# An mLSTM cell with a mixture-of-depths layer on one core: a scatter moved ahead of a weighing, a mask in halves, a shorter ranking chain, a last layer in two column halves

## The chip, the cores and the metric

The kernel runs on one core of a Trainium2 chip. The metric is the time of one execution in microseconds (us) of the device; several executions are taken and their median counts. The profile is that of one further execution.

## What is computed

The reference, cut to what matters (B = 4 batches, H = 8 heads, S = 768 positions, D = 40, F = 1024, capacity 128, all float32):

```python
for t in range(S):                       # mLSTM cell, per batch and head
    m_new = np.maximum(f_gate[:, :, t] + m, i_gate[:, :, t])
    f_stab = np.exp(f_gate[:, :, t] + m - m_new); i_stab = np.exp(i_gate[:, :, t] - m_new)
    C = f_stab * C + i_stab * outer(vt, kt);  n = f_stab * n + i_stab * kt
    y[:, :, t] = sigmoid(o_gate[:, :, t]) * (C @ qt) / np.maximum(np.abs(n @ qt), 1.0)
x = y.transpose(0, 2, 1, 3).reshape(B, S, H * D)
scores = x @ w_gate                      # mixture of depths, per batch
top_idx = np.argpartition(-scores[b], 128)[:128]
ye = np.maximum(x[b, top_idx] @ w1, 0.0) @ w2
out[b] = x[b];  out[b, top_idx] += sigmoid(scores[b, top_idx])[:, None] * ye
```

## The kernel before

**Steps.** The sequence is cut into 12 steps of 256 positions, three for a batch, numbered 0 to 11 (`N = 12`). A step holds four blocks of 64 positions: `c` is the half of 128 positions on the partitions, `r` the half of 64 within it. For each step the main loop transposes k and q on PE (`turn`, L244, copied out of PSUM by ACT), multiplies v by gate factors on POOL (`weigh`, L260: two instructions, one for `r = 0`, one for `r = 1`), forms the new states on PE (`update`, L282; added up on DVE in `states`), the scores (`scores`, L309), the masked scores on DVE (`masked`, L323), the part of the output that comes from the states (`read`, L332) and the part within a block (`attend`, L362), both into one PSUM tile `pH`. `divide` (L370) makes y on DVE, `output` (L390) multiplies it by the sigmoid of the output gate on POOL, `store` (L397) writes rows of `out`, `router` (L404) takes their score on DVE.

**The second part**, once per batch `b` when its three steps have scores: `spread` (L433) copies all 768 scores to every partition (PE, then ACT into `sb`); `compare` (L486) counts for each position how many scores are greater. Three of the six counts are made by DVE with a comparison, three by ACT with the sum of signs; `halved` (L483) turns a sum of signs s into the count (767 - s)/2. A row is chosen where its count is below 128, and its count is its place. For batches 0 to 2 `fetch` (L546) gathers the chosen rows from `out` in memory by an indirect DMA of POOL (into `xe`), `fetched` (L553) transposes them, `layer1` (with `last_rows`) and `layer2` (L600) are the two matrix products, `weighed` (L608) multiplies by the sigmoid of the score that `valued` (L565) computes, and `add` (L618) adds the result to the rows in `out` by an indirect DMA that accumulates: **the scatter**. For the last batch `picked` (L512) builds 0/1 matrices `sel_f` on DVE (count equal to place) and picks the rows by matmuls, already transposed; `fetch(3)` still gathers the plain rows, which are added on DVE, and its scatter writes without accumulating.

**Order.** It is written out by hand (`manual_schedule`): an engine executes its instructions in the order of the code. The main loop runs steps 0 to 11; at step 9 `layers` (L652) interleaves the second part of batches 0 and 1 with the step and with what step 10 needs (`weigh(10)`, `weigh(11)`, `add(0)`, `turn(10, ..)`, `update(10)`, and the ranking of batch 2). In step 10 come `numbers(2)`, `output(9, (0,))`, `fetch(2)`, `masked(10)`, `output(9, (1,))`, `update(11)`, `states(11)`, `router(9)`, `read(10)`, the transposition of q of step 11, eight sigmoids of the output gates on ACT, `attend(10)`; in step 11 `scores`, `masked`, `router(10)`, `read`, `fetched(2)`, `attend`. Behind the loop (L827 on) stand the second part of batch 2 and that of batch 3, the last scatter, and a test of flags whose register value is read on every engine. POOL's queue carries `weigh`, `output`, most stores, the gathers and the scatters; SP's carries the loads, the last of which (the output gates) are issued until 108.35 us.

A DMA on POOL's queue that touches `out` waits for earlier ones that touch the same rows: the wait of `fetch(2)` names `add(0)`, that of `add(2)` names `add(1)`, that of `fetch(3)` names `add(2)`.

Of the kernel before, what the change touches and what calls it, by code (L numbers as in the profile page):

```python
# [26 lines left out]
def _fast(ctx, tc, q, k, v, i_gate, f_gate, o_gate, w_gate, w1_in, w2_in, out):  # L27
# [105 lines left out]
    iota = const.tile([128, 128], FP, name="iota")  # L133
    id_i = const.tile([128, 2 * NS], I32, name="id_i")
# [15 lines left out]
    def tables():  # L150

        POOL.iota(iota_i, pattern=[[1, 128]], channel_multiplier=0)
        POOL.tensor_copy(out=iota, in_=iota_i)
        for c in range(2):
            POOL.iota(id_i[64 * c:64 * c + 64], pattern=[[256, NS], [64, 2]], base=128 * c, channel_multiplier=1)
        POOL.memset(ones, 1.0)
        POOL.memset(place, 1.0)
        for s in range(NS):
            POOL.memset(place[:, 2 * s:2 * s + 2, 0:1], 256.0 * s)
            POOL.tensor_copy(out=place[:, 2 * s:2 * s + 2, 1], in_=id_i[:, 0:2])  # L160
# [162 lines left out]
    def masked(n):  # L323
        P = work.tile([128, 2, 2, NP, 64], FP, name="P")
        flat = "s j c p t -> s (j c p) t"
        DVE.tensor_tensor(out=P.rearrange(flat), in0=pending[n].pop("pS").rearrange(flat), op=OP.mult,  # L326
                          in1=mask.unsqueeze(1).to_broadcast([128, 4 * NP, 64]))
        pending[n]["P"] = P

    def head(n, p, j):  # L330
        return 2 * p + j if n in APART else NP * j + p
# [30 lines left out]
    def attend(n):  # L362
        g = pending[n]
        for p in range(NP):
            for j in range(2):
                for c in range(2):
                    h = head(n, p, j)
                    g["add"](c, h, g["pH"][64 * c:64 * c + 64, h], g["P"][:, j, c, p, :], wv_t[n % 3][:, c, 2 * p + j], True)
# [62 lines left out]
    def half(b):  # L431
        return slice(128 * (b % 2), 128 * (b % 2) + 128)
# [50 lines left out]
    def halved(d):  # L483
        DVE.tensor_scalar(out=d["cnt"][:, NS:], in0=d["cnt"][:, NS:], scalar1=-0.5, scalar2=0.5 * (S - 1),
                          op0=OP.mult, op1=OP.add)
# [25 lines left out]
    def picked(b):  # L511
# [3 lines left out]
        for r in (slice(0, 3), slice(3, 6)):  # L515
            DVE.tensor_tensor(out=sel[:, r], in0=iota.unsqueeze(1).to_broadcast([128, 3, 128]),
                              in1=d["cnt"][:, r].unsqueeze(2).to_broadcast([128, 3, 128]), op=OP.is_equal)
# [47 lines left out]
    def valued(b):  # L565
        d, xe = dep[b], xe_t[b % 2]
        scr = work.tile([128, DM], FP, name="scr", bufs=1)
        sg = mod.tile([128, 1], FP, name="sg")
        DVE.tensor_tensor_reduce(out=scr, in0=xe[:, 0:DM], in1=wg, scale=1.0, scalar=0.0, op0=OP.mult, op1=OP.add,  # L569
                                 accum_out=sg)  # L570
        d["g"] = mod.tile([128, 1], FP, name="g")
        ACT.activation(out=d["g"], in_=sg, func=AF.Sigmoid)
# [34 lines left out]

    def weighed(b):  # L608

        d = dep[b]  # L610
        d["yg"] = mod.tile([128, DM], FP, name="yg")
        if b == B - 1:
            DVE.scalar_tensor_tensor(out=d["yg"], in0=d["py"], scalar=d["g"], in1=xe_t[b % 2][:, 0:DM], op0=OP.mult, op1=OP.add)
            return
        ACT.activation(out=d["yg"], in_=d["py"], func=AF.Copy, scale=d["g"])
# [48 lines left out]
    def layers(n):  # L664
# [36 lines left out]
        weigh(n + 1)  # L701
        weigh(n + 2)
        add(0)
# [135 lines left out]
    layer1(b - 1, 0)  # L839
    dep[b] = {"sb": spread(b, 0, 2 * NS, ps_u)}  # L840
# [4 lines left out]
    halved(dep[b])  # L845
    valued(b - 1)
# [17 lines left out]
    layer2(b)  # L864
    value = nc.values_load(good[0:1, 0:1], min_val=0, max_val=1)
    weighed(b)
# [353 lines left out]
```

## Time and profile before

| | |
|---|---|
| times of 3 executions | 152.1, 152.0, 151.44 us; median 152.0 us |
| the profiled execution: its own time | 150.96 us |
| its span, first to last instruction | 149.1 us |
| granted clock of TensorE, mean | 0.997 |
| busy: PE, PEld, DVE, ACT, POOL | 138.1, 121.2, 96.0, 99.5, 97.4 us |
| DMA queues' packets, share of 16 engines | SP's and ACT's 65.0%, POOL's 18.8% |

Of the span 149.1 us, 1.9 us of the execution's own time lie outside it. The times below are those of the profiled execution, counted from the start of its span. PE is the matmul side of TensorE and PEld its weight load, which overlaps it. An engine's row in the timeline merges neighbours of one kind; "[1.10 <-DVE P L326]" behind a row says how long the engine stood idle before it and whose end released it. A wait for several semaphores is named after the one that came last by the profile, which is not always the real one.

### The profile page before, as it was taken

How to read it: one execution, taken by the hardware profiler on the slowest of the kernel's cores; microseconds unless marked ns; L12 is line 12 of the kernel's file. 1: busy time of each engine (PE TensorE's matmuls, PEld its weight loads, DVE VectorE, ACT ScalarE, POOL GpSimd, SP SyncE). 2: the span in 40 equal slices, each digit the busy share in tenths (PEclk: the TensorE clock that was granted, in tenths of full speed). 3: DMA queues.
4: the chain of work that ended last, by engine and by line, in shares of the span. 5: the costliest groups of instructions: out<-in, count | busy, mean ns of one | idle time of the engine just before them, and what ended most of it. 6: DMA issues, size and time to landing. Idle time of an engine off the chain costs nothing.

```text
span 149.1 us, 6088 instructions
## 1 busy us (share of the span) xinstructions
PE 138.1 (93%) x2560; PEld 121.2 (81%) x2560; DVE 96.0 (64%) x249; ACT 99.5 (67%) x191; POOL 97.4 (65%) x128
## 2 busy tenths in 40 slices
PE   6999899999999999999999999999999799999930
PEld 7888789989879989988897986997789698799710
DVE  6469496379998597986999924562884976611010
ACT  0656864889797989997978653996977909422100
POOL 7519199969993699399986029499955669431220
PEclk9999999999999999999999999999999999999998
DMA  3999999998999899999989999999991004903101
GB/s 71 206 169 185 133 176 175 172 178 159 190 186 162 159 228 265 181 171 179 314 278 315 317 163 206 225 180 283 188 172 41 7 4 88 211 13 44 53 13 48
DMA packets 80294, 24.27 MB, mean 163 GB/s; under 512 B 75937, under 2 KB 78498, under 8 KB 80258
## 3 DMA queue, kind: packets, MB, share of 16 engines
q1 hardware_dynamic: 77568, 16.78, 65.0%
q0 software_dynamic: 2496, 6.88, 18.8%
q8 instruction: 22, 0.36, 1.1%
q10 hardware_dynamic: 194, 0.13, 0.3%
q14 instruction: 14, 0.11, 0.3%
HBM read 19.20 MB, written 4.59 MB: 160 GB/s over the span
## 4 chain that ended last, share of the span: by engine, by line
PE 39%; DMA 16%; ACT 13%; issue 10%; POOL 9%; DVE 6%; POOLq 2%; ACTq 1%; SPq 1%; DVEq 0%
PE pH L344 8%; PE pt L253 8%; PE pU L288 5%; PE py L606 4%; DMA k<-in_k_dram 4%; PE pS L320 4%; DMA xe<-out_dram,idx 4%; ACT qT L257 3%; DMA v<-in_v_dram 3%; POOL x L394 3%; DMA out_dram<-yg,idx 3%; PE pU L594 3%; DMA i_sb<-in_i_gate_dram 2%; PE ph L594 2%; ACT sgn L474 2%
## 5 line engine op out<-in xcount | busy, mean ns | idle before, releaser
L265 POOL TENSOR_TENSOR wv<-v,cols 64x656 f32<-64x656 f32 x23 | 30.9, 1345 | 15.8 <-DMA v<-in_v_dram 6.7
L394 POOL TENSOR_TENSOR x<-y,so 128x320 f32<-128x320 f32 x24 | 22.2, 934 | 5.8 <-ACT so L271 1.9
L409 DVE CUSTOM_DVE_ANT_0 scr<-x,wg 128x320 f32<-128x320 f32 x22 | 17.8, 808 | 9.0 <-POOL x L394 7.7
L271 ACT ACTIVATE so<-o 64x320 f32<-64x320 f32 x48 | 22.5, 468 | 1.0
L257 ACT COPY qT<-pt 128x512 f32<-128x512 f32 x24 | 13.8, 638 | 9.1 <-PE pt L253 9.1
L606 PE MATMUL py<-w,hT 128*128 128x320 f32 x64 | 18.2, 434 | 0.0
L288 PE MATMUL pU<-wv,k 128*64 128x82 f32 x384 | 16.5, 237 | 0.3 <-POOL wv L265 0.2
L300 DVE TENSOR_TENSOR C<-pU,C 128x164 f32<-128x164 f32 x40 | 13.1, 328 | 5.1 <-PE pU L288 3.8
L255 ACT COPY kT<-pt 128x512 f32<-128x512 f32 x24 | 13.0, 589 | 5.0 <-PE pt L253 4.7
L288 PEld LDWEIGHTS pU<-wv,k 128*64 128x64 f32 x384 | 14.5, 137 | 2.2 <-issue 1.1
L320 PE MATMUL pS<-qT,kT 40*64 40x64 f32 x768 | 14.8, 222 | 1.1 <-issue 0.6
L469 DVE TENSOR_SCALAR_CACHE_REDUCE cmp<-sb,x 128x768 f32<-128x768 f32 x12 | 12.1, 1009 | 5.4 <-ACT sb L463 5.1
L606 PEld LDWEIGHTS py<-w,hT 128*128 128x128 f32 x64 | 11.8, 190 | 4.3
L320 PEld LDWEIGHTS pS<-qT,kT 40*64 40x64 f32 x768 | 12.8, 134 | 2.7 <-issue 1.0
L344 PE MATMUL pH<-wv,P 128*64 128x82 f32 x352 | 15.0, 237 | 0.0
L326 DVE TENSOR_TENSOR P<-pS,mask 128x1024 f32<-128x1024 f32 x12 | 14.6, 1217 | 0.4 <-PE pS L320 0.4
L344 PEld LDWEIGHTS pH<-wv,P 128*64 128x64 f32 x352 | 13.2, 136 | 1.8 <-issue 1.2
L253 PE MATMUL pt<-ident,k 128*128 128x128 f32 x96 | 13.6, 280 | 0.4 <-DMA k<-in_k_dram 0.3
L401 POOL DMA_DIRECT2D out_dram<-x x22 | 13.6, 624 | 0.3 <-POOL x L394 0.3
L549 POOL DMA_INDIRECT xe<-out_dram,idx x4 | 4.4, 1095 | 14.5 <-DVE sg L569 7.8
L253 PE MATMUL pt<-ident,qw 128*128 128x128 f32 x96 | 13.0, 279 | 0.3 <-ACT qw L237 0.2
L232 ACT COPY Z<-C 64x656 f32<-64x656 f32 (+1 forms) x18 | 12.6, 698 | 0.2
(149 smaller groups left out, 244.3 us busy)
## 6 DMA issues: line engine op xcount, KB each, us to landing
k<-in_k_dram SPq DMA_DIRECT2D x24, 160.0 KB, 5.6
q<-in_q_dram SPq DMA_DIRECT2D x12, 320.0 KB, 5.5
v<-in_v_dram SPq DMA_DIRECT2D x24, 160.0 KB, 5.2
out_dram<-x POOLq DMA_DIRECT2D x22, 160.0 KB, 4.9
o<-in_o_gate_dram POOLq DMA_DIRECT2D x12, 160.0 KB, 5.6
o<-in_o_gate_dram SPq DMA_DIRECT2D x12, 160.0 KB, 4.2
w<-in_moe_w_dram SPq DMA_DIRECT2D x8, 160.0 KB, 5.8
w<-in_moe_w_dram SPq DMA_DIRECT2D x4, 256.0 KB, 5.4
```

Of the source, the lines that this page charges most:

```text
L253: PE.transpose(pt[:, p, :], src[:, c, 2 * p:2 * p + 2, :].rearrange("s j d -> s (j d)"), ident)
L257: ACT.copy(out=T.rearrange("e p (u t) -> e t p u", t=2)[:, c], in_=pt)
L265: (DVE if n == 0 and r else POOL).tensor_tensor(out=wv_t[n % 3][o, :, :, r], in0=v_t[n % NB][o], op=OP.mult, in1=cols[s][o, 0:2, b * H:b * ...
L271: ACT.activation(out=so_t[n % 3][64 * c:64 * c + 64, r], in_=o_t[n % NO][64 * r:64 * r + 64, c], func=AF.Sigmoid)
L288: PE.matmul(pU[64 * j:64 * j + 64, c, p], k_t[n % NB][:, c, 2 * p + j, :], wv_t[n % 3][:, c, 2 * p + j], start=True, stop=True)
L320: PE.matmul(pS[o, j, c, p, :], kT[e, p, t], qT[e, p, t], start=True, stop=True)
L326: DVE.tensor_tensor(out=P.rearrange(flat), in0=pending[n].pop("pS").rearrange(flat), op=OP.mult, in1=mask.unsqueeze(1).to_broadcast([128, ...
L344: PE.matmul(o, lhs, rhs, start=(c, h // 4) not in begun, stop=last, skip_group_check=True)
L394: POOL.tensor_tensor(out=x_t[b % 2][:, 2 * s + r, 0:DM], in0=pending[n]["y"][:, r].rearrange("s h d -> s (h d)"), in1=so_t[n % 3][:, r].re ...
L401: (POOL if n < N - 1 else SP).dma_start(out=out[b, a:a + 128, :].rearrange("(r t) d -> t r d", t=64), in_=x_t[b % 2][64 * c:64 * c + 64, 2 ...
L409: DVE.tensor_tensor_reduce(out=scr, in0=x[:, r, 0:DM], in1=wg, scale=1.0, scalar=0.0, op0=OP.mult, op1=OP.add, accum_out=x[:, r, DM:DM + 1])
L606: PE.matmul(d["py"], hT_t[:, f, half(b)], w2[:, f, :], start=(f == 0), stop=(f == NF - 1))
```

## The change

1. In `layers`, `add(0)` stands between `weigh(10)` and `weigh(11)` instead of behind both.
2. At step 11 the mask is multiplied in two instructions, one for the heads with `j = 0` and one for `j = 1`, and `attend` takes all heads of `j = 0` first.
3. In the last ranking `halved` is dropped: the three sums of signs are compared with a second table `margin` = 767 - 2 * place, made by one more POOL instruction at step 0, in place of `iota`. The product of `valued(2)` on DVE (gathered rows times `w_gate`) stands ahead of the comparisons instead of behind them; its sigmoid stays on ACT behind the last sum of signs.
4. `layer2` of batch 3 is computed as two halves of 160 columns in two PSUM tiles, and each half has its own multiply-and-add on DVE, which now stands ahead of the register read.

```diff
@@ tables()
         POOL.tensor_copy(out=iota, in_=iota_i)
+        POOL.tensor_scalar(out=margin, in0=iota, scalar1=-2.0, scalar2=float(S - 1), op0=OP.mult, op1=OP.add)
@@ masked(n)
-        flat = "s j c p t -> s (j c p) t"
-        DVE.tensor_tensor(out=P.rearrange(flat), in0=pending[n].pop("pS").rearrange(flat), op=OP.mult,
-                          in1=mask.unsqueeze(1).to_broadcast([128, 4 * NP, 64]))
+        flat, pS = "s j c p t -> s (j c p) t", pending[n].pop("pS")
+        for j in (slice(0, 1), slice(1, 2)) if n == N - 1 else (slice(0, 2),):
+            w = 2 * NP * (j.stop - j.start)
+            DVE.tensor_tensor(out=P[:, j].rearrange(flat), in0=pS[:, j].rearrange(flat), op=OP.mult,
+                              in1=mask.unsqueeze(1).to_broadcast([128, w, 64]))
@@ attend(n)
-        for p in range(NP):
-            for j in range(2):
-                for c in range(2):
...
+        order = [(p, j) for p in range(NP) for j in range(2)]
+        for p, j in sorted(order, key=lambda x: x[1]) if n == N - 1 else order:
+            for c in range(2):
...
@@ picked(b)
-        for r in (slice(0, 3), slice(3, 6)):
-            DVE.tensor_tensor(out=sel[:, r], in0=iota.unsqueeze(1).to_broadcast([128, 3, 128]),
+        for r, of in ((slice(0, 3), iota), (slice(3, 6), margin)):
+            DVE.tensor_tensor(out=sel[:, r], in0=of.unsqueeze(1).to_broadcast([128, 3, 128]),
                               in1=d["cnt"][:, r].unsqueeze(2).to_broadcast([128, 3, 128]), op=OP.is_equal)
@@ new function
+    def layer2_last(b):
+
+        d, w = dep[b], DM // 2
+        d["yg"] = mod.tile([128, DM], FP, name="yg")
+        for i in range(2):
+            if i == 0:
+                py = ps_t.tile([128, 512], FP, name="py", tag="t")[:, 0:w]
+            else:
+                py = ps_h.tile([128, 2, 512], FP, name="py", tag="h")[:, 0, 0:w]
+            for f in range(NF):
+                PE.matmul(py, hT_t[:, f, half(b)], w2[:, f, w * i:w * i + w], start=(f == 0), stop=(f == NF - 1))
+            DVE.scalar_tensor_tensor(out=d["yg"][:, w * i:w * i + w], in0=py, scalar=d["g"],
+                                     in1=xe_t[b % 2][:, w * i:w * i + w], op0=OP.mult, op1=OP.add)
@@ layers(n)
         weigh(n + 1)
+        add(0)
         weigh(n + 2)
-        add(0)
@@ behind the loop
     layer1(b - 1, 0)
+    total = valued(b - 1, False)
     dep[b] = {"sb": spread(b, 0, 2 * NS, ps_u)}
...
     compare(b, 5, 6)
-    halved(dep[b])
-    valued(b - 1)
+    valued_gate(b - 1, total)
...
-    layer2(b)
+    layer2_last(b)
     value = nc.values_load(good[0:1, 0:1], min_val=0, max_val=1)
-    weighed(b)
     add(b)
```

On POOL, from `weigh(10)` (wv_92) to `fetch(2)`, with the semaphores that each instruction waits for. DMASW0 to DMASW7 count the landings of POOL's own DMAs; `fetch(1)` and `fetch(2)` are on DMASW1, `add(0)` is on DMASW0. Before:

```order
L265 TENSOR_TENSOR wv_92<-v_96,cols 64x16x41 [waits DMAHW7_49,DMAHW0_49,PE_49]
L265 TENSOR_TENSOR wv_92<-v_96,cols 64x16x41 [waits DMASW1_49]
L265 TENSOR_TENSOR wv_93<-v_97,cols 64x16x41 [waits DMAHW5_49,DMAHW4_49,PE_49]
L265 TENSOR_TENSOR wv_93<-v_97,cols 64x16x41
L619 DMA out_dram<-yg,idx_1490 768x320 [waits Pool_49]
L394 TENSOR_TENSOR x_181<-y,so_102 128x320 [waits DVE_49,Activation_49]
L549 DMA xe_178<-out_dram,idx_2053 128x320 [waits DMASW4_49,DMASW3_49,DMASW5_49,DMASW2_49,DMASW6_49,DMASW0_49,DMASW7_49,DVE_49,PE_49]
```

The same place in the changed kernel:

```order
L267 TENSOR_TENSOR wv_92<-v_96,cols 64x16x41 [waits DMAHW7_49,DMAHW0_49,PE_49]
L267 TENSOR_TENSOR wv_92<-v_96,cols 64x16x41 [waits DMASW1_49]
L640 DMA out_dram<-yg,idx_1492 768x320 [waits Pool_49]
L267 TENSOR_TENSOR wv_93<-v_97,cols 64x16x41 [waits DMAHW5_49,DMAHW4_49,PE_49]
L267 TENSOR_TENSOR wv_93<-v_97,cols 64x16x41 [waits DMASW0_49]
L398 TENSOR_TENSOR x_182<-y,so_102 128x320 [waits DVE_49,Activation_49,Pool_49]
L553 DMA xe_179<-out_dram,idx_2055 128x320 [waits DMASW4_49,DMASW5_49,DMASW3_49,DMASW6_49,DMASW2_49,DMASW7_49,DVE_49,PE_49]
```

The scatter (L619, now L640) stands two weighings earlier. The wait for its landing, DMASW0, stood at `fetch(2)` and now stands at the second instruction of `weigh(11)` (wv_93).

On DVE, from the scores of step 11 (`router_last`, the ISA row on x_181) to the 0/1 matrices of the last batch. Before:

```order
L424 ISA x_181<-y,ow 128x320 [waits DVE_49,Pool_49]
L469 TENSOR_SCALAR cmp,cnt<-sb_2309,x_181 128x768 [waits Activation_49]
L469 TENSOR_SCALAR cmp,cnt<-sb_2309,x_181 128x768 [waits DVE_49] x2
L484 TENSOR_SCALAR cnt<-cnt 128x3 [waits Activation_49]
L569 ISA scr,sg<-xe_178,wg 128x320 [waits DMASW1_49]
L516 TENSOR_TENSOR sel_f<-iota,cnt 128x384 [waits DVE_49] x2
```

The same place in the changed kernel:

```order
L428 ISA x_182<-y,ow 128x320 [waits DVE_49,Pool_49]
L573 ISA scr,sg<-xe_179,wg 128x320 [waits DMASW1_49]
L473 TENSOR_SCALAR cmp,cnt<-sb_2315,x_182 128x768 [waits Activation_49]
L473 TENSOR_SCALAR cmp,cnt<-sb_2315,x_182 128x768 [waits DVE_49] x2
L520 TENSOR_TENSOR sel_f<-iota,cnt 128x384 [waits DVE_49]
L520 TENSOR_TENSOR sel_f<-margin,cnt 128x384 [waits Activation_49]
```

The halving (L484) is gone, the product for `valued(2)` (L569, now L573) stands ahead of the comparisons, and only the second of the two 0/1 matrices waits for ACT.

## Rows read from the trace of the kernel before

**Rows 1.** Timeline of PE, steps 10 and 11 and the tail: start us, us, instruction
```profile
110.05 1.35 PE L288 MATMUL pU<-wv,k 128*64 128x82 f32 x32
...
113.43 1.36 PE L344 MATMUL pH<-wv,P 128*64 128x82 f32 x32
...
118.34 1.36 PE L344 MATMUL pU<-wv,P 128*64 128x82 f32 x32 [1.10 <-DVE P L326]
119.63 1.16 PE L583 MATMUL ph<-xeT,w1c 64*128 64x128 f32 x16
...
125.05 4.47 PE L606 MATMUL py<-w,hT 128*128 128x320 f32 x16
129.36 4.15 PE L524 MATMUL pX<-sel_f,x 128*67 128x128 f32 x36
...
134.68 2.05 PE L594 MATMUL pU<-xeT,w 128*128 128x128 f32 x16
136.57 1.95 PE L594 MATMUL ph<-xeT,w 128*128 128x128 f32 x16
...
138.58 4.57 PE L606 MATMUL py<-w,hT 128*128 128x320 f32 x16
```
**Rows 2.** Timeline of DVE, the same stretch
```profile
115.14 0.49 DVE L409 CUSTOM_DVE_ANT_0 scr<-x,wg 128x320 f32<-128x320 f32 x1 [1.88 <-POOL x L394]
...
117.07 1.22 DVE L326 TENSOR_TENSOR P<-pS,mask 128x1024 f32<-128x1024 f32 x1
...
128.35 1.02 DVE L516 TENSOR_TENSOR sel_f<-iota,cnt 128x384 f32<-128x384 f32 x2
...
143.19 0.55 DVE L613 SCALAR_TENSOR_TENSOR yg<-py,g,xe 128x320 f32<-128x320 f32 x1 [4.18 <-PE py L606]
```
**Rows 3.** Timeline of POOL, steps 9 and 10 and the last gather
```profile
101.50 5.37 POOL L265 TENSOR_TENSOR wv<-v,cols 64x656 f32<-64x656 f32 x4
107.15 1.71 POOL L619 DMA_INDIRECT out_dram<-yg,idx  x1 [0.28 <-DVE C L300]
...
113.11 1.11 POOL L549 DMA_INDIRECT xe<-out_dram,idx  x1 [2.81 <-PE pt L253]
114.23 0.88 POOL L394 TENSOR_TENSOR x<-y,so 128x320 f32<-128x320 f32 x1
...
138.14 1.09 POOL L549 DMA_INDIRECT xe<-out_dram,idx  x1 [3.56 <-issue]
```
**Rows 4.** Line L549 from 104 to 116 us: waits of POOL's sequencer, ns min/median/max
```profile
L549 POOLq EVENT_SEMAPHORE  x4: 43/43/3414, 108.7 to 112.3; - x4
```
**Rows 5.** DMA issues around 107, 133 and 138 us: last number, us to landing
```profile
out_dram<-yg,idx POOLq DMA_INDIRECT x1, 5.1
...
out_dram<-yg,idx POOLq DMA_INDIRECT x1, 4.1
...
xe<-out_dram,idx POOLq DMA_INDIRECT x1, 3.1
```
**Rows 6.** Timeline of ACT between the steps' last sigmoids and the gathered rows
```profile
114.28 3.89 ACT L271 ACTIVATE so<-o 64x320 f32<-64x320 f32 x8
118.20 0.54 ACT L562 COPY xeT<-pX 64x128 f32<-64x128 f32 x2
```
**Rows 7.** Queues 106.1:107.1, 108.9:110 (SP's), 90:91.3 (POOL's): packets, MB, share of 16 engines
```profile
q1 hardware_dynamic: 441, 0.07, 42.2%
...
q1 hardware_dynamic: 1386, 0.22, 114.8%
...
q0 software_dynamic: 44, 0.16, 57.8%
```
**Rows 8.** Groups by line and shape, whole span: busy us, mean ns | idle before
```profile
L265 POOL TENSOR_TENSOR wv<-v,cols 64x656 f32<-64x656 f32 x23 | 30.9, 1345 | 15.8 <-DMA v<-in_v_dram 6.7 <-DVE cols L204 4.7 <-PE pH L344 3.6
L153 POOL CAST iota<-iota_i 128x128 f32<-128x128 int32 x1 | 0.3, 289 | 0.1
...
L300 DVE TENSOR_TENSOR C<-pU,C 128x164 f32<-128x164 f32 x40 | 13.1, 328 | 5.1 <-PE pU L288 3.8
```

More of the change, by code (lines that the diff above doesn't have):

```diff
@@ L133, in _fast @@
     iota = const.tile([128, 128], FP, name="iota")
+    margin = const.tile([128, 128], FP, name="margin")
     id_i = const.tile([128, 2 * NS], I32, name="id_i")
@@ L363, in attend @@
         g = pending[n]
-        for p in range(NP):
-            for j in range(2):
-                for c in range(2):
-                    h = head(n, p, j)
-                    g["add"](c, h, g["pH"][64 * c:64 * c + 64, h], g["P"][:, j, c, p, :], wv_t[n % 3][:, c, 2 * p + j], True)
+        order = [(p, j) for p in range(NP) for j in range(2)]
+        for p, j in sorted(order, key=lambda x: x[1]) if n == N - 1 else order:
+            for c in range(2):
+                h = head(n, p, j)
+                g["add"](c, h, g["pH"][64 * c:64 * c + 64, h], g["P"][:, j, c, p, :], wv_t[n % 3][:, c, 2 * p + j], True)
     def divide(n):
@@ L563, in fetched, with valued @@
         ACT.copy(out=d["xeT"][:, 0:2], in_=pX[:, 0:2])
-    def valued(b):
+    def valued(b, gate=True):
         d, xe = dep[b], xe_t[b % 2]
@@ L570, in valued, with valued_gate @@
                                  accum_out=sg)
+        if gate:
+            valued_gate(b, sg)
+        return sg
+    def valued_gate(b, sg):
+        d = dep[b]
         d["g"] = mod.tile([128, 1], FP, name="g")
@@ L611, in weighed @@
         d["yg"] = mod.tile([128, DM], FP, name="yg")
-        if b == B - 1:
-            DVE.scalar_tensor_tensor(out=d["yg"], in0=d["py"], scalar=d["g"], in1=xe_t[b % 2][:, 0:DM], op0=OP.mult, op1=OP.add)
-            return
         ACT.activation(out=d["yg"], in_=d["py"], func=AF.Copy, scale=d["g"])
```

## The prediction

> **What bounds the kernel now.** All four edits lie behind 101 us, so I read only that stretch, engine by engine, PE first. The timeline of PE [rows 1] shows one gap worth naming in steps 10 and 11: 1.10 us before the attention matmuls of step 11, which wait for the mask on DVE. From 118.34 us on every PE row begins where the one before ends, down to the last layer two at 138.58: the reader is to see that PE alone sets the end there. The timeline of DVE [rows 2] leads further back: the mask begins at 117.07 behind step 10's division, and that chain begins with a score product at 115.14 that waited 1.88 us for POOL. POOL's timeline [rows 3] shows why: its product at 114.23 stands behind the gather of batch 2, which began at 113.11 after 2.81 us of idleness. The row blames a PE transposition, but the sequencer's own wait, 3.41 us from 108.7 [rows 4], ends where the first scatter lands: 107.15 + 5.1 = 112.25 [rows 3, 5]. So the chain is scatter, gather, product, score, division, mask, PE. ACT runs beside it: eight sigmoids, then the copies of the gathered rows, done at 118.74 [rows 6], 0.89 us before PE first reads them at 119.63 [rows 1].
>
> **Edit 1, the scatter.** Removed: the first scatter behind four weighings. Moved: it is issued after two. The four take 5.37 us [rows 3], so two end at 101.50 + 2.69 = 104.19; with the gap of 0.28 that it has now it starts at 104.47 and its issue, 1.71 us, ends at 106.18. But the order of the changed kernel puts the wait for its landing at the second half of step 11's weighing, which had no such wait. That half takes 1.345 us [rows 8], and PE's update of step 11, at 110.05 now [rows 1], needs it; in that update's shadow stand, on PE, everything to the end. With a landing after L us the half ends at 104.47 + L + 0.05 + 1.345 and PE starts 0.05 us later (hand-overs of about 0.05 us are my choice from the gaps between neighbouring rows): PE stalls L - 4.14 us before the update.
>
> L is the unknown. The nearest rows are the same kind of scatter: 5.1 us where it is now, 4.1 us for the third one, with no other traffic [rows 5]. Below 4.1 nothing in the trace reaches for an accumulating scatter; above 5.1 the traffic of SP's loads could drive it. Now its data must go between 108.86 and 112.25, beside loads that ask for 114.8% of the engines [rows 7]; moved, its data comes due about 106.6, in a lull in which the loads take 42.2% [rows 7], before they fill up again. The gather of batch 1 also shows that POOL's packets are not starved beside loads: they took 57.8% of the engines [rows 7]. I take 4.6, the middle of the two rows: landing 109.07, second half done 110.47, PE stalled 0.46 us.
>
> What the stall meets: PE has 1.10 us of idleness ahead of step 11's attention. Moved by 0.46, the work before it ends at 118.34 - 1.10 + 0.46 = 117.70. The chain on DVE is no longer late: POOL's product ends about 110.47 + 1.0 + 1.4 + 0.9 = 113.8 (product, gather with its hand-over, product) instead of 115.11, and then PE's attention of step 10, 0.46 later than its 113.43 + 1.36 = 114.79 [rows 1], releases the division at about 115.3. Now the division begins behind the score product, about 115.55 (115.14 + 0.49 less the overlap of neighbours); so the mask starts some 0.2 earlier, at 116.85. **Edit 2** splits it: one instruction of 1.22 us becomes two; with the fixed part that a short DVE instruction shows, some 0.17 us, each is 0.17 + 1.05/2 = 0.70. The first half ends at 117.55, before PE needs it at 117.70; the second at 118.2, before PE has done the first half's heads. Bounds of edit 2: without it the mask would end at 118.05 and PE would wait 0.35 us, so it is worth 0 to 0.55, the latter if PE came early enough; it costs DVE 0.1 us, hidden behind attention.
>
> Next late is ACT: its sigmoids follow a PE transposition that is also 0.46 later, so the gathered rows are ready at 118.74 + 0.46 = 119.20, and PE goes on at about 119.25, not at 119.63. **Gain of edits 1 and 2: 0.4 us**; in general 0.85 less the stall, that is 4.99 - L: 0.85 at best, 0 at L = 5.0, a loss of 0.85 at 5.85.
>
> **Edit 3, the ranking.** Dropped on DVE: a halving (under 0.2 us) and, from this place, a product of 0.5 us. But the two 0/1 matrices are made from 128.35 to 129.37 and PE's picking begins at 129.36, directly behind a layer two that began at 125.05 and runs at its usual pace [rows 1, 2]; the first matrix is ready half a microsecond before. PE covers this: 0 taken, up to 0.3 if PE comes early by more than that half. The product now runs beside POOL's last outputs and may hold one up for its own length, 0.5 us; that ends in the last gather, which lands at 138.14 + 3.1 = 141.24 [rows 3, 5] and is needed at 143.19 [rows 2], by the first half of edit 4 at 141.0. A late gather by 0.5 still lets the second half go on time: 0. The new table is one POOL instruction, 0.29 us by the cast of the same size [rows 8], at step 0; POOL idles for loads of v after it (6.7 us in all [rows 8]): 0.
>
> **Edit 4, the last layer two.** Now 16 passes in 125.05 to 129.36, 0.269 us each at 320 columns [rows 1]; passes of 128 columns with a weight load each come every (136.57 - 134.68)/16 = 0.118 us [rows 1]. Between them, 160 columns: 0.118 + 0.151 x 32/192 = 0.143; 32 of them take 4.58 instead of 4.30: +0.28, or +0.20 with the pace of the picking, 4.15/36 = 0.115 [rows 1]. I take +0.25. The multiply-and-add behind it shrinks from 0.55 [rows 2] to about 0.35, near the 0.328 of a 164-column addition out of PSUM [rows 8]: -0.20. **Net +0.05**, between -0.05 and +0.1. The Trainium skill, "TensorE: Matmul & The Clock Gate", section "The mechanism", says that a weight load overlaps matmuls in flight only where the row groups differ; these all use all rows, and by its section "LDWEIGHTS" 128 columns cost about 107 ns, so 16 more loads would be 1.7 us, an estimate. The row at 0.118 us a pass, load included, disagrees.
>
> **Sum.** -0.40 + 0 + 0.05 = -0.35 us on the profiled execution: 150.96 becomes 150.6. The median of the runs stands 1.04 higher, at 152.0, so **151.65 us**. A measurement tells changes over 0.5%, 0.76 us, from none.
>
> **Rivals.** *The wait is free.* If the scatter lands within 4.2 us, the second half of the weighing hardly waits, the stall is nil and ACT's 0.85 us is the gain: 151.2. For it: the lull. Against: 4.1 is the row with all engines idle. The Trainium skill, "DMA: Bandwidth & Descriptors", section "Anatomy of one DMA", gives a fixed 2.0 us and bytes at 436 GB/s: 2.4 us for these 164 KB, an estimate, and the wait would be free; the scatters' rows, 4.1 and 5.1, say otherwise. Chance 0.15, and 0.07 for gains that I do not see, as a DVE chain at the tail that counted after all.
> *The wait replaces the gain.* One mechanism, on POOL between the two halves of step 11's weighing: the scatter comes into the loads' second burst (114.8% [rows 7]) and lands after 5.8 us or more, so PE stalls 1.7 us before the update, over all its cover. It decides from L = 5.0, and is measurable from 5.8: 152.9. For it: at 107.15 the scatter took 1.0 more than the idle one, though its last third ran when the loads were done. Chance 0.13.
> *Weight loads uncovered in edit 4* at one pass pitch each, 16 x 0.118 = 1.9 us: 153.5, chance 0.03.
> *The scatter isn't where the chain hung*, and edits 1 and 2 do nothing but cost a stall inside 1.10: 152.0 to 152.1, part of the 0.62 that I give to the forecast with L between 4.2 and 5.7.
>
> **How the numbers follow.** Faster 0.22, same 0.62, slower 0.16. The cases reach from 151.1 (free wait, 152.0 - 0.85 - 0.05) to 152.9 (the late scatter); the three runs of before lie 0.66 apart, and nearly all of that below their median, so I add 0.3 below: range 150.8 to 152.9.
>
> **What would show it.** The scatter starts near 104.5 and lands near 109; the second half of the weighing starts there, not at 107.5; PE shows an idle of about half a microsecond before the update of step 11, blamed on POOL, and none of 1.10 before step 11's attention; the picking still begins where layer two ends; 32 passes of 160 columns last about 4.6 us, and the last DVE instruction about 0.35. A PE gap over 1.3 us before the update would prove the forecast wrong on the slow side, none at all on the fast side.

## The result and the profile after

The changed kernel takes **153.4 us** (median of 22 executions, 151.62 to 158.6) against 151.79 for the kernel before beside it (22 executions): ratio 1.0117, 95% interval 1.0091 to 1.0144. It is 1.2% slower; 151.65 was forecast, and 153.4 lies above the range. The ratios here and below leave out executions over 1.5% above the fastest of their kernel (nine of these 22, 154.43 to 158.6 us at a mean granted clock of 0.955 to 0.979), so beside a kernel whose times fall in two groups I give the median as well. The profiled execution takes 152.92 us, its span is 151.2 us at a clock of 0.992 (before: 150.96, 149.1, 0.997).

PE's timeline, the rows that answer to [rows 1]: start us, us, instruction, and in brackets the idleness before it with what ended it.

```profile
106.58 1.35 PE L290 MATMUL pU<-wv,k 128*64 128x82 f32 x32
...
110.89 0.31 PE L547 MATMUL pi<-place,sel 128*128 128x3 bf16 x6 [0.62 <-DVE sel L501]
112.04 1.35 PE L290 MATMUL pU<-wv,k 128*64 128x82 f32 x32 [0.84 <-POOL wv L267]
...
115.42 1.36 PE L348 MATMUL pH<-wv,P 128*64 128x82 f32 x32
...
118.71 0.52 PE L563 MATMUL pX<-ident,xe 128*64 128x128 f32 x3
119.16 1.61 PE L348 MATMUL pU<-wv,P 128*64 128x82 f32 x32
120.70 1.24 PE L593 MATMUL ph<-xeT,w1c 64*128 64x128 f32 x16
...
126.20 4.47 PE L616 MATMUL py<-w,hT 128*128 128x320 f32 x16
130.51 4.15 PE L528 MATMUL pX<-sel_f,x 128*67 128x128 f32 x36
...
139.72 4.61 PE L628 MATMUL py<-w,hT 128*128 128x160 f32 x32
```

The first row is step 10's update. It began at 105.33 before, so 1.25 us were gone ahead of every edit but the new table; over the profiles of all kernels below, this row starts anywhere from 105.1 to 107.2. I therefore measure from it. The 1.10 us before step 11's attention are gone (the row at 119.16 has no idleness), an idleness of 0.84 us has come before step 11's update, blamed on POOL, and picking still begins where the layer two before it ends. The 0.62 in front of batch 2's numbers is no new cost: the matrix that it waits for begins 3.29 us after step 10's update in both kernels, and the kernel before idles 0.17 and 0.41 us in step 10's scores instead. POOL's and DVE's timelines and ACT's answer to [rows 2, 3, 6]:

```profile
102.50 2.66 POOL L267 TENSOR_TENSOR wv<-v,cols 64x656 f32<-64x656 f32 x2
105.44 1.70 POOL L640 DMA_INDIRECT out_dram<-yg,idx  x1 [0.28 <-POOL wv L267]
107.22 1.28 POOL L267 TENSOR_TENSOR wv<-v,cols 64x656 f32<-64x656 f32 x1
110.36 1.62 POOL L267 TENSOR_TENSOR wv<-v,cols 64x656 f32<-64x656 f32 x1 [1.86 <-DMA out_dram<-yg,idx]
...
113.15 1.08 POOL L553 DMA_INDIRECT xe<-out_dram,idx  x1 [0.21 <-DVE P L330]
...
145.04 1.04 POOL L640 DMA_INDIRECT out_dram<-yg,idx  x1 [4.41 <-DVE yg L629]
```

```profile
118.33 1.28 DVE L330 TENSOR_TENSOR P<-pS,mask 128x512 f32<-128x512 f32 x2
...
123.53 1.15 DVE L573 CUSTOM_DVE_ANT_0 scr<-xe,wg 128x320 f32<-128x320 f32 x1
...
144.38 0.38 DVE L629 SCALAR_TENSOR_TENSOR yg<-py,g,xe 128x160 f32<-128x160 f32 x1 [1.17 <-PE py L628]
```

```profile
116.27 3.90 ACT L273 ACTIVATE so<-o 64x320 f32<-64x320 f32 x8
120.19 0.54 ACT L566 COPY xeT<-pX 64x128 f32<-64x128 f32 x2
```

The DMA view has the landing of the first scatter and of the last (the last number, us from issue to landing):

```profile
out_dram<-yg,idx POOLq DMA_INDIRECT x1, 4.8
...
out_dram<-yg,idx POOLq DMA_INDIRECT x1, 4.3
```

The first answers to the 5.1 of [rows 5]. The last scatter of the kernel before, its row on POOL and its landing:

```profile
144.02 1.04 POOL L619 DMA_INDIRECT out_dram<-yg,idx  x1 [4.79 <-DVE yg L613]
...
out_dram<-yg,idx POOLq DMA_INDIRECT x1, 3.0
```

It took 3.0 us there. No step of the prediction looked at that number. From the start of step 10's update to the start of the last layer two the profile has 33.14 us (before: 138.58 - 105.33 = 33.25); from there to the end of the span 11.45 (before: 149.1 - 138.58 = 10.5). **So the stretch of edits 1 to 3 comes out even, and 0.9 us are lost at the end**, though PE's last work and the last multiply-and-add are as forecast.

Why the scatter is late is seen when the DMA view is cut into short windows. Three of the changed kernel: 146.4 to 146.6 us, 146.6 to 147.25, 148.2 to 148.9 (queue, packets, MB, share of 16 engines):

```profile
q8 instruction: 1, 0.02, 50.8%
...
q0 software_dynamic: 45, 0.15, 57.7%
...
q0 software_dynamic: 2, 0.01, 2.1%
```

The scatter is 48 packets, by their starts and ends three on each of 16 engines. 45 run within 0.65 us. The last three begin 0.84 us after the end of the last of these. Until then one engine carries a single packet of code that had begun 0.23 us ahead of the scatter's: 50.8% of 16 x 0.2 us is 1.63 us for its 16 KB. It ends at 148.06, and the first of the three packets begins at 148.05 (packet records).

In the kernel before, in windows 144.4 to 144.6 and 145.6 to 146.55, the code comes over a microsecond ahead of the packets, and all 48 run in one burst:

```profile
q8 instruction: 1, 0.02, 39.2%
...
q0 software_dynamic: 48, 0.16, 46.2%
```

### The profile page after: what moved, and what is told of

It is laid out like the page before. It is cut to its first block, busy times and chain, and to the rows that moved or that the text cites. A ratio compares the mean times of both kernels' runs of the same rounds, so it can differ in the third digit from the quotient of the medians.

```text
span 151.2 us, 6122 instructions
## 1 busy us (share of the span) xinstructions
PE 138.7 (92%) x2576; PEld 122.7 (81%) x2576; DVE 98.4 (65%) x250; ACT 99.7 (66%) x191; POOL 97.4 (64%) x129
## 4 chain that ended last, share of the span: by engine, by line
PE 43%; DMA 15%; POOL 12%; issue 9%; ACT 9%; DVE 6%; POOLq 1%; ACTq 1%; DVEq 0%
PE pH L348 13%; PE pt L255 11%; PE pU L290 8%; PE pS L322 6%; DMA k<-in_k_dram 5%; DMA xe<-out_dram,idx 5%; POOL wv L267 4%; POOL x L398 3%; POOL out_dram L640 3%; DMA out_dram<-yg,idx 3%; POOL out_dram L405 3%; DMA i_sb<-in_i_gate_dram 2%; ACT so L273 2%; ACT kT L257 2%; ACT qT L259 1%
## 5 line engine op out<-in xcount | busy, mean ns | idle before, releaser
L398 POOL TENSOR_TENSOR x<-y,so 128x320 f32<-128x320 f32 x24 | 21.6, 915 | 7.4 <-DVE y L390 3.0
L330 DVE TENSOR_TENSOR P<-pS,mask 128x1024 f32<-128x1024 f32 (+1 forms) x13 | 14.7, 1134 | 0.4 <-PE pS L322 0.4
L322 PE MATMUL pS<-qT,kT 40*64 40x64 f32 x768 | 14.2, 221 | 0.6 <-ACT qT L259 0.3
L616 PE MATMUL py<-w,hT 128*128 128x320 f32 x48 | 13.6, 433 | 0.0
L255 PEld LDWEIGHTS pt<-ident,k 128*128 128x128 f32 x96 | 10.3, 140 | 2.8 <-PE pS L322 1.1
```

The costliest lines, as they stand in the source:

```text
L255: PE.transpose(pt[:, p, :], src[:, c, 2 * p:2 * p + 2, :].rearrange("s j d -> s (j d)"), ident)
L322: PE.matmul(pS[o, j, c, p, :], kT[e, p, t], qT[e, p, t], start=True, stop=True)
L330: DVE.tensor_tensor(out=P[:, j].rearrange(flat), in0=pS[:, j].rearrange(flat), op=OP.mult, in1=mask.unsqueeze(1).to_broadcast([128, w, 64]))
L398: POOL.tensor_tensor(out=x_t[b % 2][:, 2 * s + r, 0:DM], in0=pending[n]["y"][:, r].rearrange("s h d -> s (h d)"), in1=so_t[n % 3][:, r].re ...
```

## The experiments

Each edit is against the changed kernel or the kernel before, as named; the ratios are against the kernel before on the same chip.

### The four edits one by one

From the kernel before, with one edit of the change each.

`e1_scatter`

```
         weigh(n + 1)
+        add(0)
         weigh(n + 2)
-        add(0)
```

> Before with edit 1 alone (the first scatter between the two weighings). Theory W (the wait that moved into step 11's weighing costs more than the gap it removes): slower than before by 1.0 to 2.0 us, so most of the changed kernel's +1.8, with a stall of 0.5 to 2 us on PE before step 11's update. Theory T (the two column halves cost the time at the end) and theory U (the new table at step 0 disturbs the loads): within 0.4 us of before, with the stall inside the gap of 1.10 that it takes the place of. My forecast's own sum: landing about 4.9 us, edit 1 between -0.1 and +0.2 us.

`e2_mask`

```
+        for j in (slice(0, 1), slice(1, 2)) if n == N - 1 else (slice(0, 2),):
...
+        for p, j in sorted(order, key=lambda x: x[1]) if n == N - 1 else order:
```

> Before with edit 2 alone (mask and attention of step 11 in halves of the heads). All three theories: 0.3 to 0.5 us faster, since attention can start on the first half at about 117.8 instead of 118.34, with DVE 0.1 us longer behind it. Slower by over 0.5 would be a fourth cause, the order of attention.

`e3_rank`

```
+        POOL.tensor_scalar(out=margin, in0=iota, scalar1=-2.0, scalar2=float(S - 1), op0=OP.mult, op1=OP.add)
...
+    total = valued(b - 1, False)
...
-    halved(dep[b])
-    valued(b - 1)
+    valued_gate(b - 1, total)
```

> Before with edit 3 alone (new table at step 0, no halving, the product of batch 2 ahead of the comparisons). Theory U: slower by 0.8 to 1.8 us, and the loss is there before 100 us (PE waits for loads of k or v that it did not wait for). Theories W and T: within 0.3 us of before, picking begins at the end of layer two as before, the last stores about 0.3 us later.

`e4_columns`

```
-    layer2(b)
+    layer2_last(b)
     value = nc.values_load(good[0:1, 0:1], min_val=0, max_val=1)
-    weighed(b)
     add(b)
```

> Before with edit 4 alone (last layer two in two column halves). Theory T: slower by 0.8 to 1.5 us, because the last scatter takes over 4 us to land (4.3 in the changed kernel, 3.0 before) or because TensorE's granted clock falls more often. Theories W and U: between -0.2 and +0.3 us; the 32 passes last 4.6 us, the last multiply-and-add 0.38, the scatter lands after 3.0 to 3.3 us.

Measured against 151.41 of before: 151.9, 151.24, 151.93 and 152.15; ratios 1.0005 [0.9957, 1.0053], 1.0011 [0.9976, 1.0046], 1.0003 [0.9964, 1.0041], 1.0000 [0.9955, 1.0046]. No edit alone carries 1.2%, and the 0.3 to 0.5 us expected of edit 2 are not seen. Of edit 4's 12 times eight are at 152.09 or above; its median is 0.74 above that of before, which its ratio does not show. But the last scatter lands after 2.8, 2.7 and 2.8 with edits 1 to 3, and after 4.5 with edit 4.

### Again, without edit 1, and with the flag read early

`r_after` is the changed kernel again, without an edit. `u1_after_but_scatter` puts the scatter back. The other two test a first theory of the late landing: that DVE's read of the flag, and its branch, now behind the multiply-and-adds, fetch code at the wrong moment.

> The changed kernel again, for a ratio on the chip on which the next three run. Theory T (the end: the last scatter takes 4.3 to 4.5 us to land, with the halved last layer two, against 2.7 to 3.0 without, because DVE's branch and the fetch of the code behind it come at the moment of the scatter's packets): last landing 4.3 to 4.5, ratio 1.006 to 1.014 against the kernel before. Theory C (the 1.2% was a chip that granted this kernel a lower clock, chance): the ratio changes with the chip and is under 1.004 here, whatever the last landing is. Theory W (the stall before the update of step 11): idle of 0.8 to 0.9 us before it again.

`u1_after_but_scatter`

```
-        add(0)
         weigh(n + 2)
+        add(0)
```

> The changed kernel with the first scatter back behind four weighings; the other three edits stay. Theory W (the wait for the landing in front of the second half of step 11's weighing is what costs): 0.8 to 1.2 us less than the changed kernel, no idle blamed on POOL before the update of step 11. Theory T (the end): the same time as the changed kernel within 0.4 us, last landing again 4.3 to 4.5 us. Theory C: as the changed kernel within the scatter of the runs, whatever its end shows.

`a1_read_ahead`, with PE's half of `layer2_last` and DVE's apart (`e4b_read_ahead`: the same ending on the kernel before)

```
     layer2_last(b)
     value = nc.values_load(good[0:1, 0:1], min_val=0, max_val=1)
+    weighed_last(b)
     add(b)
```

> The changed kernel with DVE's read of the flag that the last branch looks at ahead of the two multiply-adds, as in the kernel before, not behind them; PE's work is the same. Theory T: DVE's branch is taken and its code is fetched before the last scatter's packets run, the last scatter lands after 2.7 to 3.1 us and not 4.3 to 4.5, and the time is 1.0 to 1.5 us under the changed kernel's: ratio 0.998 to 1.004 against the kernel before. Theory W or C: no change against the changed kernel beyond 0.3 us; W has the landing at 4.3 still, if the halves themselves make it late.

> The kernel before with the halved last layer two alone, and DVE's read of the flag ahead of the two multiply-adds. Theory T: last landing 2.7 to 3.1 us (4.5 with the read behind them), so 1.2 to 1.6 us less at the end than with the halves alone as the change has them; against the kernel before -0.2 to +0.1 us, ratio 0.998 to 1.001. If the halves themselves make the scatter late (two writes of its tile, another buffer of PSUM), the landing is 4.3 to 4.5 here too and the time is 0.8 to 1.5 us over the kernel before.

Against 151.33: the repeat 153.46, 1.0114 [1.005, 1.0178]; with the early read 153.24, 1.0117 [1.0057, 1.0177], landing 4.3; `e4b` 151.95, 1.0038 [1.0006, 1.0069], landing 4.4. **Theory T falls as it stood**: the halves make the landing late wherever DVE reads the flag. Without edit 1 the landing is 4.1, and its 13 times fall in two groups, five from 150.33 to 151.59 and eight from 152.56 up (median 152.73); its ratio, 0.9993, holds hardly more than the lower one.

### Whose code it is: theory F

Queue 8, marked as instructions, carries 22 packets in every kernel, over the whole span. If they are PE's code, work on PE alone must move them.

`u4_after_but_columns` takes edit 4 back:

```
-    layer2_last(b)
+    layer2(b)
     value = nc.values_load(good[0:1, 0:1], min_val=0, max_val=1)
+    weighed(b)
```

> The changed kernel with the last layer two and its multiply-and-add undivided again; edits 1 to 3 stay. Theory F (at its end PE fetches the code behind its last branch as one packet of 16 KB, 1.0 to 1.6 us on one DMA engine; with the halves this packet stands just ahead of the last scatter's packets on that engine, and one engine's share of the scatter waits for it): the last scatter lands after 2.7 to 3.0 us and not 4.0 to 4.4, and the time is 0.7 to 1.3 us under the changed kernel's, ratio 1.002 to 1.006 against the kernel before. Theory W (what costs is the stall of 0.85 before the update of step 11 alone): no more than 0.2 us less than the changed kernel, ratio 1.010 or more.

`a2_late_fetch` (12 products, on the changed kernel) and `b2_late_fetch` (8, on the kernel before), all behind the last layer two:

```
+    pd = ps_u.tile([128, 2, 512], FP, name="pU")[:, 0, :]
+    for i in range(12):
+        PE.matmul(pd[:, 0:128], hT_t[:, 0, half(b)], w2[:, 0, 0:128], start=(i == 0), stop=(i == 12 - 1))
```

> The changed kernel with 12 more passes of 128 columns on PE behind its last pass, into a tile that nobody reads: about 1.4 us more work on PE, and nothing on the path to the last scatter. Theory F: PE's last fetch comes about 1.4 us later, behind the scatter's packets, so the scatter lands after 2.7 to 3.1 us, and the kernel is 0.6 to 1.3 us faster for having more work: ratio 1.002 to 1.007 against the kernel before. If the fetch isn't what delays the scatter: landing 4.0 to 4.4 as before, and the time the same, or up to 1 us more where PE's own end comes to set the end.

> The kernel before with 8 more passes of 128 columns on PE behind its last pass, into a tile that nobody reads, about 0.9 us. Theory F: the last fetch, which came 1.1 us ahead of the scatter's packets, now comes 0.2 us ahead of them, as in the changed kernel: landing 3.6 to 4.4 us instead of 2.7 to 3.0, time 0.6 to 1.3 us more, ratio 1.004 to 1.009. If the halves themselves are what makes the scatter late: landing 2.7 to 3.0, ratio 0.998 to 1.002.

A product is two passes, so these were 2.8 and 1.95 us of work, twice what I had reckoned, and both fetches landed elsewhere than planned. They still tell: on the kernel before, the last fetch went from 1.12 us ahead of the scatter's first packet to 1.60 behind it, past all 48; landing 2.7, ratio 0.9983 [0.9943, 1.0024], with 1.95 us more work on PE. On the changed kernel the last fetch went far behind, but the one before it slid onto the packets; landing 4.2, ratio 1.0182 [1.0127, 1.0236]. Work of 1.95 us and more on PE moves both fetches, so I take the code to be PE's. With edit 4 undone the landing is 3.1 and the ratio 1.0064 [1.0032, 1.0097].

The next two aim at the two sides: `a3_fetch_clear` has 5 products on the changed kernel, `b3_fetch_on` 3 on the one before (the first is shown against `a2_late_fetch`).

```
-    for i in range(12):
+    for i in range(5):
```

> The changed kernel with 5 more products (10 passes of 128 columns, about 1.2 us) on PE behind its last pass, into a tile that nobody reads. With 12 of them PE's last fetch but one slid onto the scatter's packets, and the last scatter landed after 4.2; 5 should put the last fetch but one 0.5 us ahead of the packets and the last one behind them. Theory F (a code fetch of PE holds up the scatter's packets on one DMA engine): landing 2.7 to 3.1 us, 0.6 to 1.0 us less time than the changed kernel, ratio 1.003 to 1.007 against the kernel before, with more work on PE. If the halves themselves make the scatter late: landing 4.0 to 4.4, ratio 1.011 or more.

> The kernel before with 3 more products (6 passes, about 0.7 us) on PE behind its last pass, into a tile that nobody reads. Theory F: the last fetch, which the kernel before makes 1.1 us ahead of the scatter's packets and the one with 8 more products 1.6 us behind them, now runs beside them: landing 3.8 to 4.5 us, 0.6 to 1.0 us more time, ratio 1.003 to 1.007. If the halves make the scatter late and not the fetch: landing 2.7 to 3.1, ratio 0.998 to 1.002.

**`a3_fetch_clear`: 151.52 us against 151.15, ratio 0.9992 [0.9956, 1.0027].** The changed kernel, with 1.28 us of useless work added to PE, lost its 1.2%; the changed kernel itself was not run again on that chip. The products alone don't speed a kernel up: `b2`, with more of them, has 0.9983. The windows of `a3` from 145.4 to 146.2 and from 146.5 to 148, the landing from the DMA view of its end, and its last POOL row:

```profile
q0 software_dynamic: 48, 0.16, 52.9%
...
q8 instruction: 1, 0.02, 5.8%
...
out_dram<-yg,idx POOLq DMA_INDIRECT x1, 2.7
```

```profile
143.84 1.04 POOL L640 DMA_INDIRECT out_dram<-yg,idx  x1 [4.54 <-DVE yg L629]
```

All 48 packets run in one burst, and the code comes behind them. `b3` missed: its fetch still began 1.10 us ahead of the packets; landing 2.8, 152.04 us, ratio 1.0014 [0.998, 1.0047]. That a fetch pushed onto the packets slows the kernel with the undivided layer two was so not shown.

From the packet records of all traces (us): the last fetch of PE from begin to end, counted from the first packet of the last scatter; how much later the last engine was done than the one before it; the landing; and the stretch from the start of the last layer two to the end of the span.

```
kernel                 fetch             last engine  landing  tail
before                 -1.12 to +0.13    0.18         3.0      10.54
e1_scatter             -1.50 to -0.52    0.16         2.8      10.66
e2_mask                -1.71 to -0.42    0.16         2.7      11.08
e3_rank                -1.21 to -0.21    0.20         2.8      10.42
u4_after_but_columns   -0.96 to +0.25    0.45         3.1      10.40
b2_late_fetch          +1.60 to +2.60    0.15         2.7      10.52
b3_fetch_on            -1.10 to -0.12    0.04         2.8      10.53
x3_before_scatter_third -1.55 to -0.47   0.15         2.7      10.58
x4_third_filled        -0.74 to +0.28    0.30         3.1      10.51
u5_filled              -1.32 to -0.34    0.15         2.7      10.50
a3_fetch_clear         +1.15 to +2.53    0.10         2.7      10.24
y1_clear_but_scatter   +1.28 to +2.50    0.17         2.8      10.27
y2_halves_clear        +1.29 to +2.51    0.02         2.8      10.27
after                  -0.23 to +1.40    1.65         4.3      11.45
r_after                -0.12 to +1.16    1.23         4.0      11.20
a1_read_ahead          -0.04 to +1.41    1.48         4.3      11.44
u1_after_but_scatter   +0.21 to +1.27    1.33         4.1      11.30
e4_columns             +0.34 to +1.82    1.64         4.5      11.65
e4b_read_ahead         -0.08 to +1.53    1.67         4.4      11.61
a2_late_fetch          +3.47 to +4.69    1.62         4.2      11.41
```

(In a2 it is the last fetch but one that meets them, -0.18 to +1.34.) Where a fetch of PE still runs 1.06 us or more after the first packet, having begun 0.34 us behind it or earlier, one engine is done 1.2 to 1.7 us late; where it ends within 0.28 us of the first packet, or begins behind all 48, 0.45 at most. No kernel is an exception, and in each of the seven late ones a packet of the last engine begins within 0.02 us of the end of the fetch. The longer tail of `e2_mask` is another thing: its packets come 7.63 us after the start of the last layer two, not 7.06, and no view names why.

### What edit 1's wait does

`x3_before_scatter_third` takes the wait away: step 11's weighing does its other half first, the scatter comes between the halves, and no weighing stands behind its landing (edit 2 is in it too).

```
         weigh(n + 1)
-        weigh(n + 2)
+        weigh(n + 2, (1,))
         add(0)
+        weigh(n + 2, (0,))
```

> The kernel before with the mask in halves, step 11's weighing in the other order of its halves, and the first scatter between them, so that no weighing waits for the landing. If the late gather is what the 1.10 us of idleness before step 11's attention came from, and the wait is what gave the gain back: the scatter starts near 105.8, the gather of batch 2 near 111.5 instead of 113.1, PE has no idle before the update of step 11 and none before step 11's attention, and the time is 0.5 to 0.9 us less than before: ratio 0.994 to 0.997, last landing 2.7 to 3.0. If the chain hung on something else: ratio 0.998 to 1.002.

It came out at 153.8 against 151.73, ratio 1.0105 [1.0046, 1.0164]. The scatter starts at 105.71, as planned, yet PE waits longer than with the wait. Its rows on POOL and DVE, then PE, then the windows from 112 to 119 (time, busy us of each engine, then granted clock, DMA share, GB/s):

```profile
107.49 1.28 POOL L265 TENSOR_TENSOR wv<-v,cols 64x656 f32<-64x656 f32 x1
108.74 0.94 POOL L396 TENSOR_TENSOR x<-y,so 128x320 f32<-128x320 f32 x1
...
108.88 0.82 DVE L486 TENSOR_SCALAR cnt<-cnt 128x3 f32<-128x3 f32 x1
109.74 0.96 DVE L499 TENSOR_TENSOR sel<-iota,cnt 128x768 bf16<-128x768 f32 x1
```

```profile
110.75 0.31 PE L545 MATMUL pi<-place,sel 128*128 128x3 bf16 x6 [1.73 <-DVE sel L499]
...
112.27 2.21 PE L346 MATMUL pH<-C,qT 40*64 40x41 f32 x64
```

```profile
112.00:113.00 1.00, 1.00 (x42) 0.91 (x42) 1.00 (x2) 0.00 (x0) 0.55 (x1) 0.72 0.06 16
113.00:119.00 6.00, 5.91 (x96) 5.18 (x93) 2.41 (x8) 3.11 (x6) 1.41 (x2) 0.50 0.10 30
```

POOL's product, come earlier, runs beside a small instruction of DVE that takes 0.16 us in the changed kernel and 0.82 here; PE stands idle for 1.73 us, and behind that its clock falls to 1.2 GHz for some 7 us, in which the row at 112.27 takes 2.21 us instead of 1.14. The Trainium skill, "SBUF — State Buffer", section "Who interferes with whom", says that such a DVE instruction and one of GpSimd can shut each other out of a shared port for its whole length; the two rows agree, as both end at 109.7.

Two kernels put idle products into PE's waits: `x4_third_filled` three into that of x3, `u5_filled` two and three into those of `u4`.

```
+                fill(pi[:, 1, 0:128], 3)
+                numbers(2, pi[:, 0, 0:3])
```

> The kernel with the first scatter between the two halves of step 11's weighing and the mask in halves, with 3 idle products (0.7 us) on PE ahead of the numbers of batch 2, where PE stood idle for 1.73 us and its granted clock then fell to 0.50 for 7 us. Theory K (the clock falls behind that idleness, and its fall is what made that kernel 1.05% slower than before): no stretch at 0.50 or one in a few executions, 1.5 to 2.5 us less than without the products, ratio 0.995 to 1.002. If the clock fell for another reason: it falls again, ratio 1.008 or more.

> The changed kernel with the last layer two undivided, and with idle products on PE in its two waits ahead of the update of step 11: 2 (0.5 us) ahead of the numbers of batch 2, 3 (0.7 us) behind them. Theory K: the profile without them had the clock at 0.50 for 3.4 us right behind the two waits; with them it stays at 1.00, and the ratio falls from 1.0064 to 0.999 to 1.004. If the clock is not what edits 1 to 3 lose by: ratio 1.005 to 1.008.

`x4`: 151.94 against 151.15, ratio 1.0045 [1.0012, 1.0079], the profile's clock at 1.00 until PE's work is done. It loses less than x3, though the intervals overlap and the gain was to be larger: DVE's small instruction takes 0.82 us there too, and PE still waits 1.05. `u5`: 152.88, 1.0078 [1.003, 1.0126], no gain: its second filling itself waited 0.70 us for DVE's flags.

The clock falls to 0.50 in other traces too, from about 112 us on and for 3 to 7 us: in `u4`, `u1`, `y1` (below) and `a2`. In the changed kernel, its repeat, `a1` and `a3` it stays at 1.00 there, although PE's waits ahead of step 11's update are those of `u4` (0.62 and 0.84), and `u1` and `y1` are without edit 1. So the fall comes in some executions and not in others. It can explain x3 in part; whether and how often it costs the changed kernel anything is not shown.

### Without edits 1 and 3, the fetch clear

`y1_clear_but_scatter` is `a3` without edit 1, `y2_halves_clear` without edits 1 and 3.

```
-        add(0)
         weigh(n + 2)
+        add(0)
...
-    total = valued(b - 1, False)
...
-    valued_gate(b - 1, total)
+    halved(dep[b])
+    valued(b - 1)
```

> The changed kernel with the first scatter back behind four weighings, and with the 5 products behind the last layer two that took the code fetch off the last scatter's packets. Theory F: landing 2.7 to 3.1 us; the time without edit 1 and without the fetch is the before kernel's or a little less, ratio 0.996 to 1.000. Theory K (the wait that edit 1 puts before the update of step 11 lets the clock fall in some executions): fewer runs over 153 us than the 3 of 12 that had edit 1 and the 5 products.

> The kernel before with the mask in halves, the last layer two in halves and the 5 products behind it: edits 2 and 4 without what went wrong with them. Theory F: landing 2.7 to 3.1 us, ratio 0.994 to 0.999 against the kernel before, and against the one with edit 3 as well the same within 0.2 us if the new table costs nothing, 0.4 to 0.8 us less if the later start of step 10 in the profiles with the new table (by 0.8 us on average) is its work and not chance.

Against 151.59: 151.41, ratio 0.9976 [0.9934, 1.0019], and 151.73, ratio 0.9980 [0.9929, 1.0032]. With the fetch clear, edits 1 and 3 make no difference that can be measured; the later start of step 10 in the profiles with the new table is not seen in the times. Theory K asked for fewer executions of `y1` over 153 us than the 3 of 12 of `a3`; there is none, but 1 of 12 in `y2`, also without edit 1: too few to tell. y1 has the lowest ratio of all, but its interval holds 1: no version here is shown to beat the kernel before.

## Why the prediction was wrong

**The step that failed** is edit 4's "Net +0.05". It priced PE's passes and the multiply-and-add, both rightly, and stopped there; the last scatter, which stands behind them and sets the end, was left at its 3.0 us without a word. It took 4.0 to 4.5. In the kernel before PE's last fetch began 1.12 us ahead of the scatter's packets and was nearly over when they came. With the halves the packets come 6.94 us after the start of the last layer two, not 7.06, and the fetch 6.71, not 5.93: the packets came 0.1 us earlier and the fetch 0.8 later, and so they met. Without products added behind it the fetch begins 5.5 to 6.3 us after that start in every trace with the undivided layer two, and 6.7 to 7.3 in every one with the halves. Why, no view shows; 16 more weight loads and passes stand before it in PE's stream.

**The size.** 0.9 us of the loss are seen in the tail of the profile, and 1.2 come back in `a3`'s (11.45 to 10.24). The runs give a3 about 1.2% against the changed kernel, 1.8 us; the rest no view shows, and the stretch ahead differs by as much between executions. Nor do all parts add up: edit 4 alone has the late landing at a ratio of 1.0000, the other three without it have 1.0064. In u4 the fetch just touched the packets (last engine 0.45 late); in which of the executions without a trace it meets them cannot be seen. That the loss goes when the fetch is moved is shown by a3, and the traces show 1.2 of its 1.8 us. What edits 1 to 3 lose without edit 4 (u4), and where the fetch falls in each execution, stays open.

**Edit 1, the stall right in kind and mis-sized, the gain behind it wrong in part.** The scatter starts at 105.44 - 1.25 = 104.19 by before's clock (forecast 104.47) and lands after 4.8, in the repeat after 4.6 (forecast 4.6). The stall is 0.84, not 0.46: the second half of the weighing took 1.62 us instead of 1.345, which is most of it. The gather came at 113.15 against 113.11 [rows 3], 1.2 us earlier if counted from step 10's update. But the chain on DVE came no earlier. PE's attention of step 10, 0.74 us later behind the stall, releases the division, at 116.82 - 1.25 = 115.57 (115.56 before), and the mask begins at 118.33 - 1.25 = 117.08 (117.07 before, forecast 116.85). Nor did ACT set the next step on: the row at 120.70 follows directly on attention, which took 1.61 us instead of 1.36. The gain of 0.4 was to appear in the stretch up to there: 14.12 us after, 14.30 before, so 0.2; the repeat had 14.86, with a wait of 0.32 more that no view names. "4.99 - L" gives 0.2 for the 4.8 that L was; that this agrees is luck, as neither its stall (0.66) nor its ACT is what the rows show.

**Edit 2** did what it was to do: 1.28 us for both halves, the first at 118.33, and PE without a wait at 119.16; in the instruction records it pauses 0.14 us within that row, until the second half is there. **Edit 3: 0** holds: 1.0003 alone, picking still begins behind layer two, and the moved product (1.15 us, where 0.5 was assumed) is hidden: DVE still waits 0.82 us for ACT's copy of the scores behind it.

**Edit 4 on PE and DVE**: 4.61 us for the 32 passes (forecast 4.58), 0.38 for the multiply-and-add (0.35). The rival of uncovered weight loads is out.

**The rivals.** "The wait replaces the gain" gave 152.9, the right side by another mechanism: its condition, a landing over 5.8 us, did not occur; taking edit 1 out leaves the late last landing (u1), and with the fetch clear it changes nothing that can be measured (y1 beside a3). The condition that I named for the slow side, a gap over 1.3 us before that update, did not occur either; the slow side had a cause at a place where no rival stood.

## What to carry over

When an edit changes the work ahead of the last transfer, in its time or its instructions, price that transfer again: look at what else the DMA engines carry at the moment at which it now comes, code included. A scatter spread over all engines lands with its slowest one, so one packet of 1.6 us on one engine is worth 1.2 us of the end. Before a change of under 1% is believed, move the suspected collision by itself: here work without use on PE made the kernel faster, which no sum of busy times could have told.

## What the runs showed of the hardware

PE's code comes as packets of 16 KB on queue 8, each 0.9 to 1.9 us on one DMA engine; two lie at the program's end, one beginning 0.5 to 2.4 us ahead of the end of PE's last row, one 0.7 to 3.1 us behind it. The Trainium skill, "Runtime: NRT & Kernel Launch", section "Instruction fetch mechanics", says that each sequencer fetches pages of 16 KiB over a DMA queue of its own, and that a taken branch outside them forces a fetch; the traces agree on size and queue, and no run here shows what a branch does. That such a packet holds up the kernel's own transfer is what these runs add.

The last scatter, which does not accumulate, lands after 2.7 to 3.1 us when nothing is in its way, the accumulating ones after 4.0 to 6.0. A DVE instruction of 0.16 us takes 0.82 beside POOL's product, DVE's product 1.15 instead of 0.48 beside POOL's outputs.
